# A host-transposed copy of x for the first stage of a spectral block: normalisation applied behind the row products

## The chip, the cores and the metric

The kernel runs on one core of a Trainium2 chip. The metric is the device time of one execution in microseconds (us), taken as the median of several runs. Five engines work from their own instruction queues: TensorE (PE in the profile; PEld are its weight loads), VectorE (DVE), ScalarE (ACT), GpSimd (POOL), and SyncE (SP), which here only issues DMAs. DMAs bring data from the chip's main memory into the on-chip buffer SBUF; matrix products land in PSUM, 8 banks of 128 x 512 fp32 numbers.

## The reference

A transformer-like block on `x` of 2048 rows of 512, all fp32. `mod` gives six vectors of 512 (shift, scale and gate of each half).

```
mod = (silu(c) @ w_mod).reshape(1, 6, 1, 512)
sa, ca, ga, sb, cb, gb = (mod[:, i] for i in range(6))
h = layernorm(x) * (1 + ca) + sa
x = x + ga * irfft2(rfft2(h) * (w_r + 1j * w_i))      # 2-D FFT over 2048 x 512
h = layernorm(x) * (1 + cb) + sb
x = x + gb * (mish(h @ w1 + b1) @ w2)                 # 512 -> 1376 -> 512
```

`layernorm` has no weights of its own: it subtracts the mean of a row and divides by the square root of its variance plus 1e-5.

## The kernel before

The Fourier transforms are products with constant matrices. Row `16 p + n` of `x` sits on partition `p` in tile `n`, so there are 16 tiles of 128 x 512. Three stages follow one another, with the dense half behind the third.

*First stage* (lines 242 to 347). Per tile: statistics on DVE (`norm_sums`, `bn_stats` and `bn_aggr`, L105 and L106); `norm_guess` adds epsilon on DVE (L111) and takes the root as Exp(-0.5 Ln) on ACT (L112, L113); `norm_refine` improves it by four small operations and forms minus mean times deviation (L118 to L126). `p1_apply` writes the normalised tile (ACT for the first three tiles, L160, else POOL, L162). `p1_turn` transposes it by four TensorE operations into a bank (L170), which ACT copies out as `ht` (L172). `p1_row` multiplies the four transposed blocks with the row matrix `krs` (L187; fp32, each counted as two instructions). ACT rounds the result to a high part `gh` (L190), DVE takes the rest `gl` (L191). `p1_split` does the same to the tile's column matrix: high part on ACT (L177), low part and negatives on POOL (L178, L179). `p1_col` is nine products of the split parts into one bank (L199 to L201), copied to `a_sb` by ACT (L202).

`krs` is the constant `kr` times one plus the scale `ca`: `scale_sums` (L207) sums `silu(c) @ w_mod` on TensorE from `wmc`, `scale_rows` (L212) multiplies on DVE. The shift `sa` goes the other way: `mod_step` (L90, L92) accumulates it on DVE from `wms`, `shift_columns` and `shift_rows` (L97, L222, L228, L230) turn it into `saz`, a correction of one column per group in the second stage. The gate `ga` is accumulated from `wmg` and multiplied into the inverse matrix `kiv` by `mod_gate` (L234, L235), the last work of the stage. `warm` (L240) runs products whose results nobody reads.

*Second stage* (lines 349 to 548). Seventeen groups of up to four frequencies: `p2_in` transposes `a_sb` (L431, copied by ACT, L434, corrected by `saz` on POOL, L436), `p2_mul` multiplies (L447), `p2_prod` multiplies by the filter `wq` on DVE (L463) and combines on POOL (L468, L469), `p2_back` transposes (L480, L483), `p2_out` multiplies (L493, L356, L357). One modulation step of the dense half (`mod_late`, twelve in all) runs on DVE in each of the rounds 1 to 12, on weights that `mod_fetch` brings two rounds ahead.

The order on each engine is the order in which the functions are called: the schedule is written by hand (`manual_schedule`). An engine works strictly in that order and waits on semaphores; SP issues its DMAs strictly in order too. Buffers come from rings: `bank` has two banks to each of four tags, `buf` two buffers to each tag; a writer waits until the last reader of the buffer it takes is done.

Of the kernel before, what the change touches and what calls it, by code (L numbers as in the profile page):

```python
# [12 lines left out]
P = 128  # L13
# [13 lines left out]
def tile_spectral_block(ctx: ExitStack, tc: tile.TileContext, x_d, w1_d, b1_d, w2_d,  # L27
                        c_d, wm_d, wq_d, wz_d, kr_d, km_d, kc_d, ki_d, kf_d, kv_d, kw_d, kp_d, out_d):
# [49 lines left out]
    wq = pw.tile([P, N2, 2, 64, 4], F32, name="wq")  # L78
# [5 lines left out]
    kw = pw.tile([32, 384], F32, name="kw")  # L84
    hring = first.enter_context(tc.tile_pool(name="hring", bufs=1))
# [30 lines left out]
    def norm_refine(lo, hi, ve, eng=nc.vector):  # L116
        r = rstd[:, lo:hi]
        eng.tensor_tensor(ve, ve, r, op=ALU.mult)  # L118
        eng.tensor_tensor(ve, ve, r, op=ALU.mult)
        eng.tensor_scalar(ve, ve, -0.5, 1.5, op0=ALU.mult, op1=ALU.add)  # L120
        eng.tensor_tensor(r, r, ve, op=ALU.mult)
        if eng is nc.vector:
            eng.scalar_tensor_tensor(nmr[:, lo:hi], mv[:, lo:hi, 0], -1.0, r, op0=ALU.mult, op1=ALU.mult)
        else:
            eng.tensor_tensor(nmr[:, lo:hi], mv[:, lo:hi, 0], r, op=ALU.mult)
            eng.tensor_scalar(nmr[:, lo:hi], nmr[:, lo:hi], -1.0, 0.0, op0=ALU.mult, op1=ALU.add)  # L126
# [30 lines left out]
    def p1_apply(n):  # L157
        h = buf(("h", "y", "t")[n % 3])
        if n < 3:
            nc.scalar.activation(h, x[:, n, :], AF.Identity, scale=rstd[:, n:n + 1], bias=nmr[:, n:n + 1])  # L160
        else:
            nc.gpsimd.tensor_scalar(h, x[:, n, :], rstd[:, n:n + 1], nmr[:, n:n + 1],  # L162
                                    op0=ALU.mult, op1=ALU.add)
        st["h", n] = h

    def p1_turn(n):
        hv = st.pop(("h", n)).rearrange("p (a b) -> p b a", b=4)
        pt = bank("A")
        for j in range(4):
            nc.tensor.transpose(pt[:, j * P:(j + 1) * P], hv[:, j, :], ident)  # L170
        ht = hring.tile([P, 4, P], F32, name="ht", tag="ht", bufs=4)
        nc.scalar.copy(ht.rearrange("p j s -> p (j s)"), pt)  # L172
        st["ht", n] = ht
# [8 lines left out]
    def p1_row(n):  # L182
        ht = st.pop(("ht", n))
        pg = bank("B")
        pgv = pg.rearrange("p (c d q) -> p d c q", c=2, d=4)
        for j in range(4):
            nc.tensor.matmul(pgv[:, j], ht[:, j, :], krs[:, j, :].rearrange("p (c q) -> p c q", c=2),  # L187
                             start=True, stop=True)
        gh, gl = buf("g1", F32R), buf("g2", F32R)
        nc.scalar.copy(gh, pg)  # L190
        nc.vector.tensor_tensor(gl, pg, plain(gh), op=ALU.subtract)  # L191
        st["g", n] = gh, gl

    def p1_col(n):
# [7 lines left out]
        nc.scalar.copy(a_sb[:, :, n, :], pa.rearrange("p (e q) -> p q e", e=8))  # L202
# [7 lines left out]
    def scale_rows(ps):  # L210
        for j in range(4):
            nc.vector.scalar_tensor_tensor(krs[:, j, :], kr[:, j, :], ps[j][:, 0:1], kr[:, j, :],  # L212
                                           op0=ALU.mult, op1=ALU.add)

# [17 lines left out]
    def mod_gate():  # L232
        ga = bank("B")
        nc.tensor.matmul(ga, ones, kr.rearrange("p j e -> p (j e)"), start=True, stop=True)  # L234
        nc.vector.tensor_tensor(kiv, kiv, ga.rearrange("p (b a) -> p b a", b=4), op=ALU.mult)  # L235

# [5 lines left out]
    with tc.manual_schedule():  # L242
        nc.scalar.dma_start(sc, c_d.rearrange("b (p k) -> p (b k)", k=4))
        for k in range(4):
            nc.scalar.dma_start(wmc[:, k, :], wm_d[:, 1, k, :])
        nc.scalar.preload_act_table_set("natural_log_exp_and_others")
        load_x(0)
        nc.sync.dma_start(ident, kp_d)
        load_x(1)
        nc.sync.dma_start(kr, kr_d)  # L250
        load_m(0)
        for n in range(2, N2):
            load_x(n)
            load_m(n - 1)
        load_m(N2 - 1)
        wmg = big.tile([P, 4, 512], F32, name="wmg", tag="cr")
        for w, i in ((wms, 0), (wmg, 2)):
            for k in range(4):
                nc.sync.dma_start(w[:, k, :], wm_d[:, i, k, :])
        nc.sync.dma_start(kf, kf_d)  # L260
        nc.sync.dma_start(wz, wz_d)
        for i in range(N2):
            nc.sync.dma_start(wq[:, i], wq_d[i])
            if i == 3:
                nc.sync.dma_start(kv, kv_d)
                nc.sync.dma_start(kw, kw_d)
# [7 lines left out]
        warm(12)  # L274
        norm_sums(0)
        norm_scale(0, 1)
        p1_apply(0)
        cps = [bank(t) for t in "DDCC"]
        for k in range(3):
            scale_sums((k,), cps)  # L280
            warm(1)
        p1_turn(0)
        scale_sums((3,), cps)
        norm_sums(1)
        ve = norm_guess(1, 2)
        norm_refine(1, 2, ve, nc.gpsimd)
        p1_split(0)
        p1_apply(1)
        scale_rows(cps)
        norm_sums(2)  # L290
        nc.sync.dma_start(kiv, ki_d)
        nc.sync.dma_start(b1n[:, 0:NF - 1], b1_d[0:(NF - 1) * P].rearrange("(f p) -> p f", p=P))
        nc.sync.dma_start(b1n[0:F - (NF - 1) * P, NF - 1:NF], b1_d[(NF - 1) * P:F].unsqueeze(1))
        p1_row(0)
        p1_turn(1)
        warm(3, "D")
        ve = norm_guess(2, 3)
        norm_refine(2, 3, ve, nc.gpsimd)
        norm_sums(3)
        p1_split(1)  # L300
        p1_row(1)
        p1_col(0)
        p1_apply(2)
        ve = norm_guess(3, 4)
        norm_refine(3, 4, ve, nc.gpsimd)
        p1_apply(3)
        norm_sums(4)
        p1_turn(2)
        p1_col(1)
        p1_split(2)  # L310
        norm_sums(5)
        norm_scale(4, 6)
        p1_turn(3)
        p1_apply(4)
        p1_apply(5)
        p1_row(2)
        p1_turn(4)
        p1_split(3)
        norm_sums(6)
        norm_sums(7)  # L320
        norm_scale(6, 8)
        p1_apply(6)
        for n in range(3, N2 + 1):
            if n < N2:
                p1_row(n)
            if n + 1 < N2:
                p1_split(n + 1)
            if n + 5 < N2:
                norm_sums(n + 5)
            if n % 2 == 0 and n + 5 < N2:  # L330
                norm_scale(n + 4, n + 6)
            if n >= 1:
                p1_col(n - 1)
            if n + 2 < N2:
                p1_turn(n + 2)
            if n + 4 < N2:
                p1_apply(n + 4)
            if 8 <= n < 12:
                mod_step(macc, wms[:, n - 8, :], n - 8, nc.vector)
            if n == 12:  # L340
                shift_columns()
            if n == 13:
                shift_rows()
            if 14 <= n < 16:
                for k in (2 * n - 28, 2 * n - 27):
                    mod_step(kr.rearrange("p j e -> p (j e)"), wmg[:, k, :], k, nc.vector)
        mod_gate()
# [532 lines left out]
```

## Time and profile before

| what | us |
|---|---|
| median of 3 runs (419.08 to 420.97) | 419.62 |
| profiled execution | 419.22 |
| its span, first to last instruction | 417.4 |
| first transposes of the second stage start at | 66.38 |
| first products of the third stage start at, about | 118.5 |

The profile is one execution. A line of a timeline reads: start, length, engine, source line, operation, output <- inputs, shape, how many were merged, and in brackets the idle time before it with what ended it. A group's line gives the count, the total busy time, the mean of one in ns, and the idle time before. Matrix products overlap in the pipeline, so their starts tell the pace better than their lengths.

### The profile page before, as it was taken

What the parts mean: (1) busy time and instruction counts of PE and PEld (TensorE: products, weight loads), DVE (VectorE), ACT (ScalarE), POOL (GpSimd) and SP (SyncE); (2) the same over time, 40 slices, a digit from 0 to 9 for tenths busy, and PEclk for the clock granted to TensorE, in tenths of its full rate; (3) what the DMA queues carried; (4) which work ended last, traced back from release to release, by engine and by line L of the source; (5) the groups of instructions that cost most, each with busy time, mean ns of one, the idle gap of its engine ahead of it and who ended that gap; (6) DMA issues with size and microseconds to landing.
All of it is one profiled execution on the core that took longest, in us unless ns stands there. A gap on an engine that the chain in (4) does not pass through costs nothing.

```text
span 417.4 us, 6112 instructions
## 1 busy us (share of the span) xinstructions
PE 404.8 (97%) x2343; PEld 350.6 (84%) x2343; DVE 185.9 (45%) x390; ACT 151.9 (36%) x338; POOL 90.1 (22%) x142
## 2 busy tenths in 40 slices
PE   8789999999999999999999999999999999999996
PEld 8679997899989999688878888878888878888874
DVE  3567855777417698635422423322423322422212
ACT  2566665467755653534311222211222211111110
POOL 0467661766503455222100000000000000000000
PEclk9999999999999999999999999999999999999999
DMA  8999520343032222111000200000200000200002
GB/s 271 332 320 344 170 77 25 103 146 160 0 94 69 70 68 80 48 53 50 19 2 0 101 2 0 2 0 0 102 0 0 2 0 2 101 0 2 0 0 101
DMA packets 18732, 30.39 MB, mean 73 GB/s; under 512 B 3472, under 2 KB 6320, under 8 KB 18448
## 3 DMA queue, kind: packets, MB, share of 16 engines
q1 hardware_dynamic: 17984, 28.96, 21.2%
q10 hardware_dynamic: 720, 1.05, 0.7%
q8 instruction: 18, 0.29, 0.3%
q14 instruction: 10, 0.08, 0.1%
HBM read 25.81 MB, written 4.19 MB: 72 GB/s over the span
## 4 chain that ended last, share of the span: by engine, by line
PE 85%; DMA 7%; DVE 3%; ACT 3%; issue 1%; POOL 1%; SPq 0%; DVEq 0%; POOLq 0%
PE bank L662 29%; PE bank L683 28%; PE bank L625 4%; PE bank L615 3%; PE bank L616 3%; PE bank L493 3%; DMA x<-in_A_x_dram 3%; PE bank L447 3%; PE bank L480 2%; PE bank L591 2%; DMA wmc<-in_w_mod_dram 1%; PE bank L431 1%; DMA wmg<-in_w_mod_dram 1%; PE bank L187 1%; PE bank L199 1%
## 5 line engine op out<-in xcount | busy, mean ns | idle before, releaser
L683 PE MATMUL bank<-w,ah 128*128 128x512 f32 (+1 forms) x352 | 108.8, 390 | 0.9 <-PE bank L662 0.9
L662 PE MATMUL bank<-h,w1h 128*128 128x512 f32 (+1 forms) x352 | 96.8, 398 | 0.0
L670 ACT ACTIVATE mw<-bank,b1n 128x512 f32<-128x512 f32 (+1 forms) x44 | 30.2, 688 | 181.2 <-PE bank L662 129.1
L671 DVE CAST ah<-mw 128x512 fp32r<-128x512 f32 (+1 forms) x44 | 20.1, 457 | 156.9 <-ACT mw L670 156.9
L683 PEld LDWEIGHTS bank<-w,ah 128*128 128x128 f32 (+1 forms) x352 | 66.1, 188 | 15.6 <-PE bank L662 1.3
L662 PEld LDWEIGHTS bank<-h,w1h 128*128 128x128 f32 (+1 forms) x352 | 65.0, 187 | 15.1
L683 PE MATMUL bank<-w,al 128*128 128x512 f32 (+1 forms) x176 | 68.6, 390 | 0.0
L662 PE MATMUL bank<-h,w1l 128*128 128x512 f32 (+1 forms) x176 | 48.2, 396 | 0.0
L662 PEld LDWEIGHTS bank<-h,w1l 128*128 128x128 f32 (+1 forms) x176 | 32.9, 187 | 8.1
L683 PEld LDWEIGHTS bank<-w,al 128*128 128x128 f32 (+1 forms) x176 | 33.0, 188 | 7.4 <-DVE al L672 0.4
L672 DVE TENSOR_TENSOR al<-mw,ah 128x512 fp32r<-128x512 f32 (+1 forms) x44 | 30.5, 692 | 4.5 <-PE bank L683 0.5
L615 PE MATMUL bank<-kc,d 128*128 128x128 f32 x128 | 24.9, 276 | 0.5 <-ACT d L356 0.5
L616 PE MATMUL bank<-kc,d 128*128 128x128 f32 x128 | 24.7, 275 | 0.0
L463 DVE TENSOR_TENSOR buf<-bank,wq 128x512 f32<-128x512 f32 (+1 forms) x32 | 20.2, 674 | 8.8 <-POOL buf L469 4.1
L105 DVE BATCH_NORM_STATS2 st<-x 128x6 f32<-128x512 f32 x32 | 22.0, 687 | 0.4
L638 POOL TENSOR_TENSOR buf<-buf,modr 128x512 f32<-128x512 f32 (+1 forms) x11 | 14.2, 1289 | 33.0 <-DMA buf<-in_B_w_dram 28.8
L571 POOL TENSOR_TENSOR w1l<-buf,w1h 128x512 fp32r<-128x512 f32 (+1 forms) x12 | 14.4, 1201 | 29.1 <-ACT w1h L570 29.0
L199 PE MATMUL bank<-buf,mring 128*128 128x512 f32 x48 | 20.3, 422 | 0.0
L615 PEld LDWEIGHTS bank<-kc,d 128*128 128x128 f32 x128 | 19.4, 192 | 0.7 <-ACT d L356 0.7
L616 PEld LDWEIGHTS bank<-kc,d 128*128 128x128 f32 x128 | 19.4, 192 | 0.0
L187 PE MATMUL bank<-modr,ht 128*128 128x128 f32 x128 | 17.4, 279 | 0.2 <-ACT ht L172 0.2
L625 PE MATMUL bank<-kiv,buf 128*128 128x128 f32 x128 | 17.2, 277 | 0.0
(141 smaller groups left out, 567.3 us busy)
## 6 DMA issues: line engine op xcount, KB each, us to landing
buf<-in_B_w_dram SPq DMA_DIRECT2D x18, 256.0 KB, 2.6
x<-in_A_x_dram SPq DMA_DIRECT2D x16, 256.0 KB, 4.4
wq<-in_w_q_dram SPq DMA_DIRECT2D x16, 256.0 KB, 4.9
out_dram<-x SPq DMA_DIRECT2D x16, 256.0 KB, 2.1
wm<-in_w_mod_dram SPq DMA_DIRECT2D x12, 256.0 KB, 2.8
mraw<-in_km_dram SPq DMA_DIRECT2D x16, 128.0 KB, 4.4
kc<-in_kc_dram SPq DMA_DIRECT2D x2, 1024.0 KB, 6.7
wmc<-in_w_mod_dram ACTq DMA_DIRECT2D x4, 256.0 KB, 6.0
```

Of the source, the lines that this page charges most:

```text
L105: nc.vector.bn_stats(t, x[:, n, :])
L187: nc.tensor.matmul(pgv[:, j], ht[:, j, :], krs[:, j, :].rearrange("p (c q) -> p c q", c=2), start=True, stop=True)
L199: nc.tensor.matmul(pa, m[:, a, 0:128], g, start=(i == 0), stop=False)
L463: nc.vector.tensor_tensor(tv, pbv, wt.unsqueeze(1).to_broadcast([P, 2, 64, nq]), op=ALU.mult)
L615: nc.tensor.matmul(o, dj[:, 0:128], kc[0][:, n, :], start=True, stop=False)
L616: nc.tensor.matmul(o, dj[:, 64:192], kc[1][:, n, :], start=False, stop=True)
L625: nc.tensor.matmul(px[:, j * P:(j + 1) * P], e[:, j * P:(j + 1) * P], kiv[:, j, :], start=True, stop=True)
L662: nc.tensor.matmul(ps, w[:, k, fs], h[:, k, :], start=(i == 0), stop=(i == 11))
L670: nc.scalar.activation(w, ps, AF.Mish, bias=b1n[:rows, g % NF:g % NF + 1])
L671: nc.vector.tensor_copy(ah, w)
L672: nc.vector.tensor_tensor(al, w, plain(ah), op=ALU.subtract)
L683: nc.tensor.matmul(out_ps[b][j], a[:, j * P:(j + 1) * P], w2[f // 6][:rows, f % 6, w, :], start=(f == 0 and i == 0), stop=(f == NF - 1 and ...
```

## The change

The host hands over a second copy of `x`, `x_t`, in which each tile is already transposed (16 tiles of 128 x 4 x 128). Row products run on that raw copy. Mean and deviation, which belong to a row of `x` and so to a partition of the result, are applied behind the product: `row_sums` forms once the row products of ones, `kb`; per tile DVE computes `c = kb * mean - product` (`p1_mean`), ACT `gh = c * r` rounded, and DVE `gl = c * r - gh` (`p1_low`), with `r` the deviation taken with a minus sign (`p1_scale`). The statistics still read the untransposed tile. Transposes, their copies and the applies are gone. Row products run two tiles ahead of column products, and the copy to `a_sb` (`p1_save`) is called one tile later.

Around it: the transposed tiles stand in a ring of eight (`xring`), and loads of tile `n + 10` are called behind the row products of tile `n + 2`; the second half of the filter (`wqb`) takes the ring's memory and is loaded at the start of the second stage; constants of the second stage are loaded after tile 15 (`load_rest`); `wmc` comes in two DMAs instead of four, `wms` in one instead of four. The shift is accumulated by ACT and POOL (`shift_sum`) instead of DVE; `shift_rows` stands behind the last tile. The gate `ga` and `mod_gate` move into the second stage, whose modulation steps are now sixteen, some rounds with two; its first two `p2_mul` are called later (behind six and seven `p2_in` instead of three and four), and DVE does the subtraction of `p2_prod` for the first three and the last two groups, POOL every addition.

```
-    wq = pw.tile([P, N2, 2, 64, 4], F32, name="wq")
+    wqa = pw.tile([P, 8, 2, 64, 4], F32, name="wqa")
+    xring = pw.tile([P, 8, 4, P], F32, name="xring", tag="half")
+    kb = modr[:, 2]
...
+    def p1_scale(lo, hi, eng):
+        ve = norm_guess(lo, hi)
         r = rstd[:, lo:hi]
         eng.tensor_tensor(ve, ve, r, op=ALU.mult)
         eng.tensor_tensor(ve, ve, r, op=ALU.mult)
+        eng.tensor_scalar(ve, ve, 0.5, -1.5, op0=ALU.mult, op1=ALU.add)
         eng.tensor_tensor(r, r, ve, op=ALU.mult)
...
-    def p1_apply(n):
-    def p1_turn(n):
...
+    def load_xt(n):
+        t = xring[:, n % 8]
+        nc.sync.dma_start(t, xt_d[n])
+        st["xt", n] = t
+    def load_all(n):
+        load_xt(n)
+        load_x(n)
+        load_m(n)
+    def load_rest():
+        nc.sync.dma_start(ident, kp_d)
+        nc.sync.dma_start(kf, kf_d)
+        nc.sync.dma_start(wz, wz_d)
+        for i in range(8):
+            nc.sync.dma_start(wqa[:, i], wq_d[i])
+            if i == 2:
...
+    def row_products(pg, data):
         pgv = pg.rearrange("p (c d q) -> p d c q", c=2, d=4)
         for j in range(4):
+            nc.tensor.matmul(pgv[:, j], data(j), krs[:, j, :].rearrange("p (c q) -> p c q", c=2),
                              start=True, stop=True)
+    def p1_row(n):
+        xt = st.pop(("xt", n))
+        st["pg", n] = pg = bank("AB"[n % 2])
+        row_products(pg, lambda j: xt[:, j, :])
+    def row_sums():
+        ps = bank("D")
+        row_products(ps, lambda j: ones)
+        nc.scalar.copy(kb, ps)
+    def p1_mean(n):
+        c = buf("hy"[n % 2])
+        nc.vector.scalar_tensor_tensor(c, kb, mv[:, n, 0:1], st.pop(("pg", n)), op0=ALU.mult, op1=ALU.subtract)
+        gh = buf("g1", F32R)
+        nc.scalar.activation(gh, c, AF.Copy, scale=rstd[:, n:n + 1])
+        st["g", n] = c, gh
+    def p1_low(n):
+        c, gh = st.pop(("g", n))
+        gl = buf("g2", F32R)
+        nc.vector.scalar_tensor_tensor(gl, c, rstd[:, n:n + 1], plain(gh), op0=ALU.mult, op1=ALU.subtract)
         st["g", n] = gh, gl
...
+    def shift_sum(k):
+        t = macc if k == 0 else buf("t")
+        nc.scalar.activation(t, wms[:, k, :], AF.Copy, scale=sc[:, k:k + 1])
+        if k:
+            nc.gpsimd.tensor_tensor(macc, macc, t, op=ALU.add)
...
+        load_xt(0)
+        nc.sync.dma_start(kr, kr_d)
         load_x(0)
         load_m(0)
+        for n in range(1, 8):
+            load_all(n)
...
+        warm(14)
         norm_sums(0)
+        p1_scale(0, 1, nc.vector)
         cps = [bank(t) for t in "DDCC"]
+        for k in range(4):
             scale_sums((k,), cps)
+            if k == 1:
+                warm(4)
+        scale_rows(cps)
+        p1_split(0)
+        p1_row(0)
+        load_all(8)
+        row_sums()
+        p1_row(1)
+        load_all(9)
         norm_sums(1)
+        p1_scale(1, 2, nc.gpsimd)
+        p1_mean(0)
         p1_split(1)
         p1_split(2)
+        for n in range(N2):
+            if n >= 1:
+                p1_save(n - 1)
+            if n + 2 < N2:
+                p1_row(n + 2)
+                if n + 10 < N2:
+                    load_all(n + 10)
+                if n == 4:
+                    nc.sync.dma_start(wms, wm_d[:, 0, :, :])
+                if n == 6:
+                    load_rest()
             if n + 1 < N2:
+                p1_mean(n + 1)
+            p1_low(n)
+            if n == N2 - 1:
                 shift_columns()
+            p1_col(n)
+            if n + 3 < N2:
+                p1_split(n + 3)
+            if n == 0:
+                norm_sums(2)
+            if n + 3 < N2:
+                norm_sums(n + 3)
+                if n % 2 == 0:
+                    p1_scale(n + 2, n + 4, nc.gpsimd if n else nc.vector)
+            if 10 <= n < 14:
+                shift_sum(n - 10)
+        p1_save(N2 - 1)
+        shift_rows()
...
-        eng = nc.vector if g == seq[-1] else nc.gpsimd
+        eng = nc.vector if g in (*seq[:3], *seq[-2:]) else nc.gpsimd
         eng.tensor_tensor(y[:, 0:u], pr[0][:, 0:u], pr[1][:, u:w], op=ALU.subtract)
-        eng.tensor_tensor(y[:, u:w], pr[0][:, u:w], pr[1][:, 0:u], op=ALU.add)
+        nc.gpsimd.tensor_tensor(y[:, u:w], pr[0][:, u:w], pr[1][:, 0:u], op=ALU.add)
...
+    when = (3, 4, 5, 6, 6, 7, 8, 9, 9, 10, 11, 12, 12, 13, 14, 15)
+    for i, s in enumerate(when):
+        work_mod[s].append((i // 4, (0, 1, 0, 2)[i // 4], nc.vector, i % 4))
...
+        for i in range(8):
+            nc.sync.dma_start(wqb[:, i], wq_d[8 + i])
         for i in range(LEAD):
             p2_in(seq[i])
-            if i in (2, 3):
-                p2_mul(seq[i - 2])
+            if i in (5, 6):
+                p2_mul(seq[i - 5])
...
+            if s == 7:
+                mod_gate()
```

More of the change, by code (lines that the diff above doesn't have):

```diff
@@ L155, in load_x @@
         nc.sync.dma_start(x[:, n:n + 1, :], xv[:, n:n + 1, :])
-    def p1_apply(n):
[L158 to L164, printed above, removed]
-    def p1_turn(n):
[L167 to L173, printed above, removed]
+    def load_xt(n):
[13 more added lines that the diff above has]
+            if i == 2:
+                nc.sync.dma_start(kv, kv_d)
+                nc.sync.dma_start(kw, kw_d)
+                nc.sync.dma_start(kiv, ki_d)
+                nc.sync.dma_start(b1n[:, 0:NF - 1], b1_d[0:(NF - 1) * P].rearrange("(f p) -> p f", p=P))
+                nc.sync.dma_start(b1n[0:F - (NF - 1) * P, NF - 1:NF], b1_d[(NF - 1) * P:F].unsqueeze(1))
     def p1_split(n):
@@ L519, in mod_shift, with mod_gate @@
             nc.scalar.copy(cols[:, 1, i, :], ps[:, 0:4])
+    def mod_gate():
+        ga = bank("A")
+        nc.tensor.matmul(ga, ones, modr[:, 0], start=True, stop=True)
+        nc.vector.tensor_tensor(kiv, kiv, ga.rearrange("p (b a) -> p b a", b=4), op=ALU.mult)
     kc = []
+    wqb = pw.tile([P, 8, 2, 64, 4], F32, name="wqb", tag="half")
     with tc.manual_schedule():
[L523 removed]
+        for i in range(8):
+            nc.sync.dma_start(wqb[:, i], wq_d[8 + i])
         for i in range(LEAD):
             p2_in(seq[i])
[L526 to L527 removed]
+            if i in (5, 6):
+                p2_mul(seq[i - 5])
         for s in range(len(seq) + 3):
```

140 lines of the change are left out of this document (22 added, 118 removed).

## The prediction

> **What bounds the kernel now.** I read the page first, then the stretches of the first 32 us, then TensorE's timeline through the first stage. From the page:
>
> ```profile
> span 417.4 us, 6112 instructions
> PE 404.8 (97%) x2343; PEld 350.6 (84%) x2343; DVE 185.9 (45%) x390; ACT 151.9 (36%) x338; POOL 90.1 (22%) x142
> x<-in_A_x_dram SPq DMA_DIRECT2D x16, 256.0 KB, 4.4
> mraw<-in_km_dram SPq DMA_DIRECT2D x16, 128.0 KB, 4.4
> ```
>
> TensorE is busy 97% of the span, so time is won only where its work shrinks or where it stands idle. The busy time of each engine in stretches of 4 us (first column: the stretch, its length; last two: DMA share, GB/s):
>
> ```profile
> 12.00:16.00 4.00, 2.45 (x19) 2.07 (x18) 2.25 (x6) 2.22 (x7) 2.08 (x8) 1.00 0.93 320
> 16.00:20.00 4.00, 2.61 (x19) 2.27 (x19) 2.64 (x9) 2.48 (x7) 2.25 (x8) 1.00 1.02 354
> 20.00:24.00 4.00, 3.32 (x25) 2.96 (x24) 0.89 (x4) 2.37 (x6) 2.97 (x9) 1.00 0.97 328
> 24.00:28.00 4.00, 2.75 (x21) 2.49 (x20) 3.36 (x9) 1.50 (x4) 2.35 (x4) 1.00 0.93 296
> 28.00:32.00 4.00, 4.00 (x33) 3.82 (x32) 3.37 (x10) 2.93 (x8) 2.76 (x5) 1.00 1.01 366
> ```
>
> From 12 to 28 us TensorE is idle 4.87 us of 16; from 28 on it is full. Its timeline, with one tile of the full part and the end of the stage:
>
> ```profile
> 21.58 0.28 PE L201 MATMUL bank<-buf,mring 128*128 128x256 f32 x1
> ...
> 28.32 0.65 PE L170 MATMUL bank<-ident,buf 128*128 128x128 f32 x4
> 28.82 1.06 PE L187 MATMUL bank<-modr,ht 128*128 128x128 f32 x8
> 29.63 0.48 PE L199 MATMUL bank<-buf,mring 128*128 128x512 f32 x1
> ...
> 31.12 0.65 PE L170 MATMUL bank<-ident,buf 128*128 128x128 f32 x4
> ...
> 54.62 0.95 PE L97 MATMUL bank<-ones,modr 128*128 128x1 f32 x8
> 55.44 1.14 PE L187 MATMUL bank<-modr,ht 128*128 128x128 f32 x8
> ...
> 58.32 1.06 PE L222 MATMUL bank<-kr,cols 128*128 128x128 f32 x8
> 59.21 1.06 PE L187 MATMUL bank<-modr,ht 128*128 128x128 f32 x8
> ...
> 65.42 1.12 PE L234 MATMUL bank<-kr,ones 128*128 128x512 f32 x2
> 66.38 1.72 PE L431 MATMUL bank<-ident,a_sb 128*128 128x128 f32 x11
> ```
>
> Tile 1's column products end at about 21.8, tile 2's only at 28.3; then a tile takes 2.80 us (28.32 to 31.12): transposes 0.50, row products 0.81, column products 1.49. The second stage starts at 66.38. Reading starts, not busy times, matters: the ends overlap.
>
> **Start.** The shift is worked from these rows:
>
> ```profile
> 6.35 1.52 PE L207 MATMUL bank<-sc,wmc 128*128 128x128 f32 x8
> ...
> 10.63 1.06 PE L207 MATMUL bank<-sc,wmc 128*128 128x128 f32 x8
> 11.06 1.16 DVE L212 SCALAR_TENSOR_TENSOR modr<-kr,bank 128x128 f32<-128x128 f32 x4 [1.39 <-PE bank L207]
> 11.84 0.19 POOL L118 TENSOR_TENSOR ve<-ve,rstd 128x1 f32<-128x1 f32 x1 [11.38 <-ACT rstd L113]
> 12.11 0.19 POOL L119 TENSOR_TENSOR ve<-ve,rstd 128x1 f32<-128x1 f32 x1
> ```
>
> The modulation sums still start near 6.35. Transposes no longer stand among them, but four warm products do; the 1 MB of `wmc` and the 0.78 MB ahead of `mraw` on SP come at 0.33 MB/us, hence by 8 to 9.5. I take 10.6 for the first `scale_rows` (0.5 earlier; bounds 10.2 to 11.3). Row products of tile 0 end at 12.1, `row_sums` (new, another 0.9) at 13.0, its ACT copy to `kb` at 13.8. Then `c(0)` on DVE to 14.5, `gh(0)` on ACT to 15.4, `gl(0)` to 16.15; statistics of tiles 2 and 3 to 17.75, `ve`, Ln and Exp (0.2 each, L113 below, and two hand-overs) to 18.55, four refining operations on DVE at 0.2 (POOL's start 0.27 apart) to 19.4 and `c(2)`, `gl(1)` to 20.8. Column products of tile 1 end 0.6 later, 21.4: no better than now. But rows and means run ahead, so the hole of tile 2 (21.8 to 28.3) is not repeated.
>
> **The steady tile.** TensorE keeps 0.81 + 1.49 = 2.30 us. DVE gets two products a tile for one; POOL loses the apply, ACT the copy of the transposes. From DVE's timeline, the answer on line 111 (shortest, median, longest ns) and the groups of the stage (busy, then mean ns of one):
>
> ```profile
> 29.92 0.68 DVE L105 BATCH_NORM_STATS2 st<-x 128x6 f32<-128x512 f32 x1
> 30.63 0.18 DVE L106 BATCH_NORM_AGGREGATE mv<-st 128x2 f32<-128x6 f32 x1
> 30.73 0.66 DVE L191 TENSOR_TENSOR buf<-bank,buf 128x512 fp32r<-128x512 f32 x1
> 31.30 0.68 DVE L105 BATCH_NORM_STATS2 st<-x 128x6 f32<-128x512 f32 x1
> ...
> 51.61 0.74 DVE L92 SCALAR_TENSOR_TENSOR modr<-wms,sc,modr 128x512 f32<-128x512 f32 x1
> 52.28 0.68 DVE L191 TENSOR_TENSOR buf<-bank,buf 128x512 fp32r<-128x512 f32 x1
> ```
> ```profile
> L111 DVE TENSOR_SCALAR ve<-mv x15: 142/170/700, 7.1 to 169.5; 128x2 f32<-128x2 f32 x8, 128x1 f32<-128x1 f32 x4, 128x4 f32<-128x4 f32 x3
> ```
> ```profile
> L178 POOL TENSOR_TENSOR mring<-mraw,mring 128x256 fp32r<-128x256 f32 x16 | 12.3, 766 | 4.8 <-ACT mring L177 4.8
> L202 ACT COPY a_sb<-bank 128x512 f32<-128x512 f32 x16 | 9.4, 588 | 4.5 <-PE bank L201 4.4
> L177 ACT CAST mring<-mraw 128x256 fp32r<-128x256 f32 x16 | 6.8, 424 | 0.0
> L179 POOL TENSOR_SCALAR mring<-mring 128x256 fp32r<-128x256 f32 x16 | 6.6, 411 | 1.5
> L113 ACT ACTIVATE rstd<-rstd 128x2 f32<-128x2 f32 x6 | 1.2, 204 | 0.2
> L160 ACT ACTIVATE buf<-x,nmr,rstd 128x512 f32<-128x512 f32 x3 | 2.4, 815 | 2.4 <-POOL nmr L126 1.4 <-DVE nmr L123 1.0
> ```
>
> By starts: statistics 0.81 (29.92 to 30.73). `c`, a scalar-tensor-tensor with one PSUM input, between 0.57 (L191) and 0.67 (L92): 0.62. `gl`, two SBUF inputs, 0.67 undisturbed, up to the 0.85 of the mean in the second stage (row below): 0.70. `ve` once a pair, 0.14 to 0.70: 0.2 a tile. Sum 2.33, bounds 2.1 to 2.7. ACT: 0.59 + 0.82 (L160 bounds `gh` above, L202 below) + 0.42 + 0.2 = 2.0, with `shift_sum` on tiles 10 to 13 up to 2.9, absorbed because `gh` is a tile ahead of `gl`. POOL: 0.77 + 0.41 + 0.55 = 1.7. DVE and TensorE are level, so they will miss each other at times: I take 2.45 a tile (2.30 to 2.8). The pair's loop of the deviation, statistics to `ve` to ACT (0.5) to four POOL operations at 0.27 (11.84 to 12.11) to `gh` to `gl`, sums to 0.81 + 0.4 + 0.6 + 1.1 + 0.9 + 0.7 = 4.5 against 4.9 for two tiles: it just fits.
>
> **End of the stage.** `gl(12)` ends at 20.8 + 11 x 2.45 = 47.75, its columns 0.6 later; tile 13 takes 2.30, tile 14 (no row left) 1.49, `shift_columns` 0.82 (54.62 to 55.44) and tile 15 1.49: 54.45. `shift_rows` is moved behind it, 0.89 (58.32 to 59.21), and covers the last save. Second stage at 55.4, so 66.38 - 55.4 = **11.0 us won**. With 2.30 and 2.8 a tile: 12.6 and 7.1.
>
> **Second stage.** `mod_gate` is moved, not removed: 0.96 (65.42 to 66.38) comes back between full products. Four more modulation steps go to DVE:
>
> ```profile
> 80.00:84.00 4.00, 4.00 (x38) 4.00 (x37) 2.51 (x5) 2.53 (x8) 1.15 (x4) 1.00 0.28 78
> L92 DVE SCALAR_TENSOR_TENSOR modr<-wm,sc,modr 128x512 f32<-128x512 f32 x9 | 7.6, 849 | 0.0
> ```
>
> TensorE is full there and DVE has 1.5 us free in 4, so the 4 x 0.85 and the differences moved from POOL are mostly hidden; groups with two steps are not quite, and I charge 0.5 (0 to 2). The fill starts with six groups of transposes before its first product, paced by the ACT copies, and its waits for `saz` (reductions now just ahead) are covered by them; the subtraction on DVE takes POOL's turn out. I take these as even (-1 to +1).
>
> **Queues.** SP now carries per tile 0.64 MB (two rows of 256 KB, one of 128), 1.95 us at 0.33 MB/us: below 2.45, and eight tiles are issued before the ring makes SP wait for a row product. Tile 3 lands near 14, needed at 17. `wms` (1 MB) and the 2.8 MB behind it follow tile 15's load at about 30 and land by 42. The eight `wqb` loads wait for the last row product (near 49), 2 MB, by 58; behind them on SP stand only fetches needed after 62, and `wqb` itself is read after 75. All this is off the path; a delay of one tile at the start would cost 2.
>
> The sum: -11.0 + 0.96 + 0.5 = **-9.5**. The profiled execution took 419.22, 1.8 outside its span; that is 0.4 under the median, 419.62, from which I subtract: **410.1**.
>
> **A rule against it.** L111 takes 0.14 at its shortest and 0.70 at its longest: something holds DVE up. The Trainium skill, "SBUF — State Buffer", section "Who interferes with whom", says that a VectorE operation with two SBUF inputs and a GpSimd operation that reads SBUF exclude each other for a whole instruction; until now the low part had one input in PSUM, now both are in SBUF. By L92, which has such inputs and takes 0.74 in the first stage and 0.85 on average in the second, the trace shows little of it; its price is the first rival's.
>
> **Rivals.** (1) *DVE and POOL block each other.* `gl` waits each time for the POOL operation in progress: half of 0.77, or all of it. A tile becomes 2.8 to 3.1, times 12 tiles: +4 to +8, **414 to 418**. For: L111's 0.70. Against: L92's means. (2) *Slower: the deviation loop becomes the period.* If `ve` is held 0.7, POOL's four operations queue behind a split (1.18) and `gh` behind a save and a cast (1.0), the loop is 4.5 + 0.3 + 1.2 + 1.0 = 7.0 a pair: 3.5 a tile, 12 x 1.05 = +12.6, **422.7**. It decides from 6.6 a pair on. Against: those operations are issued in an order in which the split goes first. (3) *TensorE alone bounds*, 2.30 a tile and an even fill: **408**. (4) *It does not do what it says*: the second stage is not ready earlier, because `saz`, `ident` or the late loads hold it; then the 11 us turn into a wait at its door and the time stays within 2 us, **419**. Against: the loads end by 42 at the rate shown.
>
> **Chances.** Forecast (408.5 to 413) 0.57; rival 1 0.20; rival 3 0.09; rival 4 0.05; rival 2 0.09. A measurement here tells 0.5% (2.1 us) from no change. Faster takes the forecast, rival 3 and most of rival 1: 0.84; same 0.07; slower 0.09. The range, 407.3 to 416.0, takes in rival 3 and three quarters of rival 1 and leaves out the rest of it and rivals 2 and 4: 0.19. The forecast's own is 408.5 to 413.
>
> **What would show it.** Right: no transposes before the second stage, whose first one starts at 55 to 56; TensorE's column products of tile 2 end before 25; a tile of 2.3 to 2.5 with DVE about 95% busy; `gl` near 0.72. Wrong: `gl` or L178's successor over 0.9 (rival 1); ACT waiting on POOL for `gh` in every pair (rival 2); TensorE idle 2 us or more between the last column product and the first transposes (rival 4); the start of the first row product after 12.

## The result and the profile after

The changed kernel takes **417.73 us** in the median of twenty executions (414.65 to 419.40); the kernel before took 419.16 on the same chips. The ratio, which goes by averages and not by the two medians, is 0.9951, with an interval of 0.9936 to 0.9967: a gain clear of the noise but small, 1.4 us by the medians, where 9.5 were forecast.

The execution that was profiled is the fastest of the twenty, 414.65 us. So there are two questions: why this one won 4.6 us and not 9.5, and why most executions are 3 us longer than it. First the page of the changed kernel, and its engines in stretches of 4 us (columns as before, the granted clock third from the end):

```profile
span 412.7 us, 5968 instructions
PE 397.7 (96%) x2287; PEld 343.1 (83%) x2287; DVE 192.1 (47%) x377; ACT 146.3 (35%) x322; POOL 87.6 (21%) x139
```
```profile
20.00:24.00 4.00, 2.94 (x21) 2.77 (x22) 3.93 (x8) 2.62 (x5) 1.55 (x3) 1.00 0.99 347
24.00:28.00 4.00, 4.00 (x31) 3.77 (x31) 3.93 (x9) 2.57 (x7) 2.45 (x7) 1.00 1.01 364
...
52.00:56.00 4.00, 1.90 (x12) 1.53 (x10) 1.25 (x2) 2.27 (x4) 3.37 (x8) 1.00 0.94 284
```

TensorE lost 7.1 us of work (404.8 to 397.7), and looks full from 24 us on instead of 28. But a new gap stands at the end of the stage, in 52 to 56, and POOL is the busiest engine there. TensorE's timeline names the places:

```profile
10.90 1.26 PE L196 MATMUL bank<-modr,xring 128*128 128x128 f32 x8
...
21.06 0.50 PE L227 MATMUL bank<-buf,mring 128*128 128x512 f32 x1 [2.28 <-DVE buf L219]
...
21.63 1.05 PE L196 MATMUL bank<-modr,xring 128*128 128x128 f32 x8
...
23.93 1.05 PE L196 MATMUL bank<-modr,xring 128*128 128x128 f32 x8
...
33.83 1.05 PE L196 MATMUL bank<-modr,xring 128*128 128x128 f32 x8
...
39.05 1.05 PE L196 MATMUL bank<-modr,xring 128*128 128x128 f32 x8
...
54.50 0.50 PE L227 MATMUL bank<-buf,mring 128*128 128x512 f32 x1 [2.10 <-ACT buf L213]
...
56.65 1.05 PE L99 MATMUL bank<-ones,modr 128*128 128x1 f32 x8 [0.39 <-POOL modr L250]
...
59.06 1.05 PE L259 MATMUL bank<-kr,cols 128*128 128x128 f32 x8
59.95 2.27 PE L424 MATMUL bank<-ident,a_sb 128*128 128x128 f32 x15
```

The start is as forecast: row products from 10.90, a hole of 2.28 at tile 1, none at tile 2. The first tiles then take 2.30 to 2.37 each (21.63 to 23.93 is one). From the column products of tile 6 on, a pair of tiles takes 5.22 us (33.83 to 39.05 is one), not 4.6 or 4.9; the busy time hides this, since the ends overlap the waits, and the starts tell it. Tile 14 waits 2.10 us. The second stage starts at 59.95: 6.4 us won in place of 11.0.

**The loop that sets 5.22.** All engines through one pair, from a `gh` that waits for POOL to the next such `gh`, and on to the next `ve`:

```profile
31.53 0.72 ACT L213 ACTIVATE buf<-buf,rstd 128x512 fp32r<-128x512 f32 x1 [1.65 <-POOL rstd L132]
...
32.16 0.39 ACT L188 CAST mring<-mraw 128x256 fp32r<-128x256 f32 x1
...
32.62 1.01 POOL L189 TENSOR_TENSOR mring<-mraw,mring 128x256 fp32r<-128x256 f32 x1 [1.13 <-ACT mring L188]
...
33.73 0.41 POOL L190 TENSOR_SCALAR mring<-mring 128x256 fp32r<-128x256 f32 x1
...
33.89 0.26 DVE L113 TENSOR_SCALAR ve<-mv 128x2 f32<-128x2 f32 x1
...
34.10 0.73 POOL L189 TENSOR_TENSOR mring<-mraw,mring 128x256 fp32r<-128x256 f32 x1
...
34.43 0.20 ACT L115 ACTIVATE rstd<-rstd 128x2 f32<-128x2 f32 x1
...
34.72 0.74 DVE L219 SCALAR_TENSOR_TENSOR buf<-buf,rstd 128x512 fp32r<-128x512 f32 x1
...
34.92 0.81 POOL L190 TENSOR_SCALAR mring<-mring 128x256 fp32r<-128x256 f32 x1
...
35.69 0.19 POOL L129 TENSOR_TENSOR ve<-ve,rstd 128x2 f32<-128x2 f32 x1
...
36.53 0.20 POOL L132 TENSOR_TENSOR rstd<-rstd,ve 128x2 f32<-128x2 f32 x1
...
36.76 0.72 ACT L213 ACTIVATE buf<-buf,rstd 128x512 fp32r<-128x512 f32 x1 [1.65 <-POOL rstd L132]
...
37.51 0.75 DVE L219 SCALAR_TENSOR_TENSOR buf<-buf,rstd 128x512 fp32r<-128x512 f32 x1 [0.60 <-ACT buf L213]
...
38.18 0.69 DVE L107 BATCH_NORM_STATS2 st<-x 128x6 f32<-128x512 f32 x1
...
39.12 0.26 DVE L113 TENSOR_SCALAR ve<-mv 128x2 f32<-128x2 f32 x1
```

Read first the ring that the deviation goes round: `ve` 33.89, root on ACT done at 34.63, four operations on POOL from 35.69 to 36.73, `gh` at 36.76, `gl` at 37.51, statistics at 38.18, the next `ve` at 39.12. That is 5.23 us, and 1.06 of it is the stretch from 34.63 to 35.69, in which POOL still works on the split (L189, L190) that stands ahead of the four operations in its queue. A ring with a wait in it does not set the pace. The one without runs through POOL: `gh` at 31.53, the cast behind it on ACT at 32.16, the first split of the pair on POOL at 32.62 (it had waited for that cast), the second at 34.10, the four operations from 35.69, and the next `gh` at 36.76, 5.23 later. Two queues close it: the cast stands behind `gh` on ACT, and the four operations stand behind both splits on POOL.

Two of its operations are stretched while a `gl` runs on DVE (at 34.72, and by the timeline at 32.29): L189 takes 1.01 against 0.73 at 34.10, L190 takes 0.81 against 0.41 at 33.73. Without these 0.68 us the ring would be 4.55 by these rows, an estimate, just under the 4.59 of two tiles on TensorE. So the order of the queues and the stretching set the 5.23 together.

**The end.** POOL and ACT ahead of `gh(14)`:

```profile
49.77 1.29 POOL L250 TENSOR_TENSOR modr<-modr,buf 128x512 f32<-128x512 f32 x1
51.01 1.20 POOL L189 TENSOR_TENSOR mring<-mraw,mring 128x256 fp32r<-128x256 f32 x1
52.30 0.41 POOL L190 TENSOR_SCALAR mring<-mring 128x256 fp32r<-128x256 f32 x1
52.66 0.20 POOL L129 TENSOR_TENSOR ve<-ve,rstd 128x2 f32<-128x2 f32 x1
```

The deviation of tile 14 is ready on ACT at 50.56 (L115 there, by the timeline); POOL reaches it at 52.66, behind an addition of `shift_sum` (L250, 1.29) and a split lengthened to 1.20. By the timeline 6.53 us pass from `gh(12)` (47.20) to `gh(14)` (53.73), 1.30 more than the ring's 5.23: one addition. The rest of the hole is the ring's own, since TensorE has no row products left to do between these tiles and arrives earlier.

### The profile page after: what moved, and what is told of

Its sections match the earlier page's. It is cut to its first block, busy times and chain, and to the rows that moved or that the text cites. A ratio compares the mean times of both kernels' runs of the same rounds, so it can differ in the third digit from the quotient of the medians.

```text
span 412.7 us, 5968 instructions
## 1 busy us (share of the span) xinstructions
PE 397.7 (96%) x2287; PEld 343.1 (83%) x2287; DVE 192.1 (47%) x377; ACT 146.3 (35%) x322; POOL 87.6 (21%) x139
## 4 chain that ended last, share of the span: by engine, by line
PE 87%; DVE 4%; POOL 3%; issue 2%; ACT 1%; DMA 1%; POOLq 0%
PE bank L664 30%; PE bank L685 29%; PE bank L627 4%; PE bank L617 4%; PE bank L618 3%; PE bank L440 3%; PE bank L486 3%; PE bank L593 2%; PE bank L473 2%; PE bank L272 2%; PE bank L424 1%; PE bank L196 1%; POOL mring L189 1%; DVE buf L456 1%; POOL mring L190 1%
## 5 line engine op out<-in xcount | busy, mean ns | idle before, releaser
L227 PE MATMUL bank<-buf,mring 128*128 128x512 f32 x48 | 20.8, 433 | 6.4 <-ACT buf L213 3.9
L189 POOL TENSOR_TENSOR mring<-mraw,mring 128x256 fp32r<-128x256 f32 x16 | 13.9, 867 | 18.0 <-ACT mring L188 18.0
L196 PE MATMUL bank<-modr,xring 128*128 128x128 f32 x128 | 16.9, 276 | 0.0
```

Source lines behind the costliest of these rows:

```text
L189: nc.gpsimd.tensor_tensor(m[:, 1, 0:256], mraw[:, n, :], plain(m[:, 0, 0:256]), op=ALU.subtract)
L196: nc.tensor.matmul(pgv[:, j], data(j), krs[:, j, :].rearrange("p (c q) -> p c q", c=2), start=True, stop=True)
L227: nc.tensor.matmul(pa, m[:, a, 0:128], g, start=(i == 0), stop=False)
```

## The experiments

All kernels but the unaltered one are edits of the changed kernel; each was compared with the kernel before on its chip. Ratios are to that kernel.

**Unaltered, twice.** Edit: none.

> The changed kernel once more, unaltered. Its profiled execution (414.65) is the fastest of twenty whose median is 417.73; that of before lies at its own median. Theory D (data arrive late in typical executions): a typical execution shows the same pace of tiles from 30 us on, but a longer wait for x tiles or their transposed copies ahead of it, or a second stage that waits for wqb or wm. Theory J (the loop itself jitters): the same arrivals, but pairs of tiles longer than 5.2 us or a longer stall ahead of tile 14's column products (2.1 in the profile shown). Expected 417 to 418 by both; the profile tells which.

> The changed kernel unaltered, beside the next three on one chip. Theory C (holes lower the clock): median 416 to 418, mean clock mostly 0.984 to 0.996, times rising as the clock falls. Rival H (chips differ, filling does nothing): the same times as the kernels with filled holes on this chip, within 0.6 us.

The first gave 415.96 us (414.67 to 420.36, ten executions), ratio 0.9932 (0.9900 to 0.9963); the second, on another chip, 417.56 (415.37 to 417.81, seven), ratio 0.9953 (0.9935 to 0.9970). Both have pairs of 5.22 us, so theory J falls. Of theory D the first one's profile (415.69) shows a start that waits for data, with row products 0.6 us later (11.50); the typical execution of the second has not even that (10.53). What goes with the time from one execution to the next is the mean granted clock of TensorE: in the first, 414.7 at 0.999 to 1.000, 415.7 to 416.0 at 0.995, 416.9 to 417.9 at 0.986 to 0.988, 420.4 at 0.984. The twenty of the result line up in the same way: 414.65 at 0.999, a cluster of 417.3 to 417.9 mostly at 0.985 to 0.986. The kernel before has no such cluster; the means of its executions stand at 0.994 to 1.000. The stretches of the second, whose profile is a typical execution (417.56):

```profile
20.00:24.00 4.00, 3.28 (x16) 3.05 (x17) 3.90 (x10) 2.62 (x5) 1.87 (x3) 0.72 1.05 371
24.00:28.00 4.00, 4.00 (x28) 3.77 (x27) 3.86 (x8) 2.35 (x6) 2.46 (x6) 0.86 1.04 338
...
56.00:60.00 4.00, 4.00 (x16) 3.60 (x16) 1.35 (x2) 1.25 (x3) 0.94 (x1) 0.50 0.96 347
60.00:64.00 4.00, 3.87 (x22) 3.44 (x21) 0.85 (x2) 1.14 (x3) 0.00 (x0) 0.66 0.40 153
```

Right behind each of the two holes (2.28 us to 20.72 and 2.11 us to 54.83 in this timeline) the clock falls, to half at the lowest, and TensorE passes 16 products in 56 to 60, where the next kernel below passes 26 at full clock. Its second stage starts at 62.92, which is 52.39 us behind its first row products, against 49.05 in the fastest execution (59.95 and 10.90). A theory that holes cost only their own length has no place for this.

**The holes filled with unread products.** Both holes:

```
             for i, (a, g) in enumerate(...)       # inside p1_col
+                if n == 1 and i == 2:
+                    warm(9, "D")
...
+            if n == 14:
+                warm(9, "D")
             p1_col(n)
```

> The changed kernel with nine products nobody reads in each of its two holes of over 2 us (ahead of the last third of tile 1's column products and ahead of tile 14's). Theory C (the holes lower the granted clock in part of the executions, which costs the 3 us between the fastest execution, 414.65, and the median, 417.73): the mean granted clock is 0.997 or more in every execution, all of them end at 414.3 to 415.5, the fastest is not faster. Rival D (arrival of data, clock only an accompaniment): the clock rises but the times stay spread, median above 416.5.

> Both holes filled, as before on another chip. Theory C: median 414.2 to 415.2, clock 0.997 or more in nearly all executions, 1.5 to 3 us below the unaltered kernel on the same chip. Rival H: within 0.6 us of it.

414.48 us (414.21 to 414.68), ratio 0.9892 (0.9877 to 0.9907), and beside the unaltered kernel on the same chip 414.72 (414.18 to 414.97), ratio 0.9893 (0.9880 to 0.9906): 2.8 us below that one's 417.56, with intervals that do not touch. Its stretches:

```profile
20.00:24.00 4.00, 3.72 (x30) 3.40 (x29) 3.93 (x9) 2.43 (x5) 1.28 (x3) 1.00 0.96 318
...
56.00:60.00 4.00, 3.58 (x26) 3.17 (x25) 1.44 (x3) 1.65 (x5) 1.31 (x1) 1.00 0.87 300
```

The clock was 0.998 to 1.000 in all eight executions of the two runs, though the second stage started no earlier than in the profiled execution of the result: 49.06 us behind the first row products, against 49.05. So work that nobody reads buys 2.8 us: the clock is the cause of the distance between the fastest and the usual execution.

**One hole alone**, by two sizes of filler: the first hole by nine products (or five and four in two banks), the late one likewise.

> Products nobody reads only in the late hole (ahead of tile 14), the hole of tile 1 as it is. By theory C each hole costs where it meets the clock's decision. If the late hole is the dear one, since the end of the stage and the second stage's start follow it: clock 0.995 or more in nearly all executions, median 414.5 to 415.2. If the hole of tile 1 is the dear one: clock 0.985 to 0.996 as before, median above 416.

> Only the hole of tile 1 filled. Theory C with the late hole as the dear one: clock 0.985 to 0.996, median within 0.7 us of the unaltered kernel. With the early hole as the dear one: median 1 us or more below it.

> Only the hole ahead of tile 14 filled (the kernel whose median was 418.15 on another chip). With the late hole as the dear one: 1 us or more below the unaltered kernel here, so that the 418.15 was the chip's; else within 0.7 us of it or above.

> Only the hole of tile 1 filled, but by two takings of a bank (five and four products), so that the rotation of the two D banks behind it is that of the unaltered kernel and of the one with both holes filled. If the rotation made the wait at the head of the dense half (2.8 to 3.1 us with one taking, 0.9 to 1.4 with none or two), it is back under 1.5. Then the cost of the late hole alone shows: median 415.5 to 417, clock 0.992 to 0.996 in those executions that lose. If not, the wait stays near 3 and the median above 417.5.

> Only the hole ahead of tile 14 filled, again by two takings. Same test of the rotation: wait at the dense half under 1.5. Then the cost of the early hole alone: median 415 to 416, clock about 0.996 in those executions that lose (3 to 4 us at a lower clock around 20 to 28 us).

The late one: 418.15 (ratio 0.9967, 0.9954 to 0.9981), again 417.50 (0.9959, 0.9946 to 0.9973), with five and four 418.29 (0.9959, 0.9940 to 0.9979). The first: 418.53 (0.9988, 0.9963 to 1.0014), with five and four 418.65 (0.9968, 0.9940 to 0.9996). None gained on the unaltered kernel (417.56 on the chip of the runs with 417.50 and 418.53). The profiles show why they can't be read as prices of one hole: all five have a new wait of 2.8 to 3.2 us at the head of the dense half (near 168 us), with a drop of the clock behind it, where the result's profile waits 1.4 and the kernel with both filled 0.9 and 1.1. With the first hole filled:

```profile
PE bank L687 <- issue: 2.8, 1, 2.8
```
```profile
168.00:172.00 4.00, 1.17 (x4) 0.63 (x3) 2.54 (x8) 2.82 (x5) 1.27 (x1) 0.86 0.14 54
```

The runs with five and four products tried the idea that an odd number of banks taken shifts the later rotation; the wait stayed, so that idea falls. The timelines show what is late there: the fourth of POOL's products with the gate of the dense half (L642 in this kernel) comes after a wait of 2.2 to 2.7 us in all five, and of 1.1 to 1.6 in the unaltered kernels and those with both holes filled. Behind it stand a cast on ACT, a split and the next statistics on DVE, and then on ACT the root and a table load of 1.28, ahead of the activation that TensorE waits for. Why that product is late is open.

The price of each hole by itself these kernels don't give, but for one execution a timeline does. In the typical one (417.56), counted from the first row products and set against the fastest, 1.6 us are lost right behind the first hole, of which 0.7 are left at the column products of tile 10, since tiles that wait for POOL take in the rest. Another 2.65 are lost from there to the second stage, behind the late hole.

**The shift back on DVE.**

```
-                shift_sum(n - 10)
+                mod_step(macc, wms[:, n - 10, :], n - 10, nc.vector)
```

> The shift is accumulated on DVE again (four steps at the same places), POOL's three additions and ACT's four scalings go. Theory Q (POOL's queue): the additions of 1.3 us delay the last splits and deviations, so the 2.1 us stall before tile 14 and most of the wait before shift_columns go, and the second stage starts 2.5 to 3.5 us earlier: ratio to before lower by 0.006 to 0.008 than the unaltered kernel's. Theory P (port exclusion alone): DVE's own steps have two SBUF inputs as well, so about as much is lost to them: within 0.002 of the unaltered kernel.

414.63 us (414.30 to 416.07), ratio 0.9893 (0.9856 to 0.9929). Pairs stay at 5.22. Its first row product came 0.8 late in the profiled execution (11.69), its second stage at 59.85: 0.9 earlier against that start, well under the 2.5 to 3.5 of theory Q. The interval overlaps that of the unaltered kernel on the same chip (0.9900 to 0.9963), so the gain over it is not clear by the times. The hole at tile 14 falls from 2.10 to 0.74, but DVE, with another modulation step in each of four tiles, now holds up two more (0.67 and 0.63). The addition moves from one full engine to another.

**The split behind the deviation.**

```
             p1_col(n)
             if n + 3 < N2:
-                p1_split(n + 3)
...
                     p1_scale(n + 2, n + 4, nc.gpsimd if n else nc.vector)
+                p1_split(n + 3)
```

> p1_split(n+3) is called behind p1_scale, so POOL does the deviation ahead of the split of that round. Theory Q: two tiles fall from 5.22 us to DVE's own 4.6 to 4.8, five pairs, 2 to 3 us earlier second stage. Theory P: gl and the splits still exclude each other, two tiles stay above 5.0, gain under 0.7 us.

415.67 us (413.98 to 417.12), ratio 0.9909 (0.9876 to 0.9942), which again overlaps the unaltered kernel's; the pace of the tiles tells more. Its timeline of TensorE and the groups of its first 60 us, which are set against those of the next experiment:

```profile
36.61 1.05 PE L196 MATMUL bank<-modr,xring 128*128 128x128 f32 x8
...
38.91 1.05 PE L196 MATMUL bank<-modr,xring 128*128 128x128 f32 x8
...
55.02 1.48 PE L99 MATMUL bank<-ones,modr 128*128 128x1 f32 x8 [2.08 <-POOL modr L250]
```
```profile
L189 POOL TENSOR_TENSOR mring<-mraw,mring 128x256 fp32r<-128x256 f32 x16 | 14.3, 894 | 11.1 <-ACT mring L188 11.1
...
L219 DVE SCALAR_TENSOR_TENSOR buf<-buf,rstd 128x512 fp32r<-128x512 f32 x16 | 13.5, 846 | 1.9 <-ACT buf L213 1.0 <-PE bank L229 0.8
```

With four small operations no longer behind a split, tiles take 2.30 to the end of the loop, although the stretched operations stay long: without this order there is no pair of 5.22. (That it takes the stretching as well shows in the next experiment.) The end of the stage does not profit: the additions pile up on POOL instead, `shift_columns` waits 2.08 for them, and behind that wait the clock of this execution is 0.50 (56 to 60). Its second stage starts at 60.77, with a lower clock behind the first hole too (0.67 in 20 to 24); the execution to hold it against is the typical one of the unaltered kernel, with 62.92.

**`c` in PSUM.**

```
-        c = buf("hy"[n % 2])
+        c = bank("D")
```

> c is written to PSUM (the two banks of tag D, idle in the loop) instead of SBUF, so gl has one SBUF input. Theory P: gl falls from a mean of 0.81 to 0.70, POOL's low product from 0.87 to 0.75 and its negation from 0.51 to 0.41, two tiles from 5.2 to 4.7 us; the second stage starts 1.5 to 3 us earlier. Theory Q: the durations may fall, but the order on POOL stays, two tiles stay within 0.3 us of 5.2, and the stall at tile 14 stays above 1.5.

411.52 us (411.03 to 413.99), ratio 0.9824 (0.9781 to 0.9867), clear of the unaltered kernel's on the same chip (415.96 us there). `gl` now has one input in SBUF and one in PSUM. The groups of the first 60 us, of the result and of this kernel:

```profile
L189 POOL TENSOR_TENSOR mring<-mraw,mring 128x256 fp32r<-128x256 f32 x16 | 13.9, 867 | 18.0 <-ACT mring L188 18.0
L219 DVE SCALAR_TENSOR_TENSOR buf<-buf,rstd 128x512 fp32r<-128x512 f32 x16 | 13.0, 811 | 5.5 <-ACT buf L213 5.3
...
L190 POOL TENSOR_SCALAR mring<-mring 128x256 fp32r<-128x256 f32 x16 | 8.1, 507 | 1.4
...
L113 DVE TENSOR_SCALAR ve<-mv 128x2 f32<-128x2 f32 (+1 forms) x9 | 2.1, 228 | 0.3
```
```profile
L219 DVE SCALAR_TENSOR_TENSOR buf<-bank,rstd,buf 128x512 fp32r<-128x512 f32 x16 | 11.9, 743 | 1.8 <-ACT buf L213 1.7
L189 POOL TENSOR_TENSOR mring<-mraw,mring 128x256 fp32r<-128x256 f32 x16 | 11.8, 735 | 18.1 <-ACT mring L188 17.6
...
L190 POOL TENSOR_SCALAR mring<-mring 128x256 fp32r<-128x256 f32 x16 | 6.5, 408 | 1.4
...
L113 DVE TENSOR_SCALAR ve<-mv 128x2 f32<-128x2 f32 (+1 forms) x9 | 4.1, 455 | 0.3
```

One edit of DVE's input takes 0.13 us off POOL's first split operation, 0.10 off the second and 0.07 off `gl`: the two engines had held each other up. `ve` now meets the split instead and doubles. The order of the queues is unaltered here, and still pairs take 4.81 (35.58 to 40.39 in its timeline), the holes at the end are 0.32, 0.83 and 0.36, and the second stage starts at 56.71.

**Both together, and the shift with them.** Shift on DVE and late split; then `c` in PSUM with these; then late split, `c` in PSUM and `shift_sum` on POOL two tiles earlier (`if 8 <= n < 12: shift_sum(n - 8)`):

> Both edits on the order of POOL together: the split behind the deviation, and the shift accumulated by DVE; c stays in SBUF. Theory Q (POOL's queue is the whole of the late second stage): pairs of tiles at 4.6 us, no stall over 1 us after tile 2, second stage at 56 to 57, median 411 to 413. Theory P (the exclusion by itself keeps it late): DVE, with two operations of two SBUF inputs a tile in the last tiles, falls behind, second stage after 58.5, median above 414.

> The same two edits and c in PSUM. If queue and exclusion are two parts of one loop, either remedy already brings the pair to 4.6 to 4.8 and the second adds at most 1 us: second stage at 55 to 56.5, median 410 to 411.5. If they are separate costs the gains add: median below 409.5.

> Split behind the deviation, c in PSUM, and the shift still summed by ACT and POOL but two tiles earlier (tiles 8 to 11). By the account of the last tiles (POOL's additions of 1.3 us delay the last deviations and shift_columns) no stall over 1 us is left behind tile 2 and TensorE bounds: pairs at 4.6, second stage at 55 to 56, median 409.5 to 411. If DVE is the bound instead, pairs stay at 4.8 and the second stage starts at 56 to 57.

411.67 us (ratio 0.9822, 0.9807 to 0.9837), 410.96 (0.9825, 0.9796 to 0.9855) and 410.57 (0.9800, 0.9785 to 0.9815), with second stages at 56.50, 56.13 and 56.41. Pairs are 4.59 in all three, which is two tiles of TensorE; in the last a hole of 1.37 stays at tile 14, where none over 1 us was expected. The remedies do not add: each takes a part out of one ring, and once the ring is shorter than 4.6 us the rest of its waits cost nothing.

**The shift earlier, alone.**

> The changed kernel with one edit: shift_sum on tiles 8 to 11 instead of 10 to 13. If POOL's additions delay the last deviations, the 2.1 us stall ahead of tile 14 and the wait ahead of shift_columns go, and the second stage starts 2 to 3 us after where c in PSUM and the late split have it: near 57.5 to 58.5, with pairs of tiles still at 5.2 or longer where the additions now fall. If the last tiles are held by something else, it stays at 59.5 to 60.

418.27 us (417.30 to 419.06), ratio 0.9970 (0.9957 to 0.9983): a miss. The stalls come earlier (1.21 us at tile 12, 2.11 at tile 14), the second stage at 63.98, with the clock at 0.64 and 0.50 in 56 to 64. In a ring that POOL's queue already sets, there is no tile in which the additions are free; in the kernel with the late split and `c` in PSUM the pairs stay at 4.59 with the additions on the same tiles.

**One more step on the best.** Late split, `c` in PSUM, earlier shift, and the statistics of tile 2 ahead of the first `c`:

```
+        norm_sums(2)
         p1_mean(0)
...
-            if n == 0:
-                norm_sums(2)
```

> The best kernel so far (c in PSUM, split behind the deviation, shift on tiles 8 to 11) with the statistics of tile 2 ahead of the first c, where DVE waits 1.1 us for kb. If that wait takes them in, the hole of tile 1 shrinks by 0.8 us and so does the time: median 409.6 to 410.0. If x tile 2 has not landed by 13 us, or the first c is pushed back, no gain: 410.4 to 410.8.

**410.30 us** (409.94 to 411.72), ratio 0.9794 (0.9774 to 0.9814): the lowest median of all, below both kernels, though not to be told from the 410.57 of the kernel that it edits (another chip, overlapping intervals). The hole of tile 1 is 1.95 us where that kernel has 2.43, 0.5 less and not 0.8. Its rows keep their pace nearly to the end of the stage:

```profile
23.74 1.05 PE L196 MATMUL bank<-modr,xring 128*128 128x128 f32 x8
...
42.09 1.05 PE L196 MATMUL bank<-modr,xring 128*128 128x128 f32 x8
...
50.79 0.50 PE L227 MATMUL bank<-buf,mring 128*128 128x512 f32 x1 [1.38 <-ACT buf L213]
...
55.50 2.27 PE L422 MATMUL bank<-ident,a_sb 128*128 128x128 f32 x15
```

Eight tiles from 23.74 to 42.09 are 2.29 each.

## Why the prediction was right and wrong

**Right: the direction, the start, what is full.** First `scale_rows` at 10.44 by the timeline (10.6 said), row products of tile 0 done at 12.00 (12.1), `gl(1)` at 20.26 to 20.9 (20.8), no second hole, tiles of 2.30 where nothing else holds, `gh` and `gl` near their prices. `mod_gate` took 0.96 by starts, as said. The second stage lasted 53.4 us (59.95 to 113.35) for 52.1 before, 1.3 more for the 1.46 charged.

**Wrong: "it just fits".** The step that failed is the deviation loop of a pair, summed to 4.5 us against 4.9. Its terms were not short: without the wait for POOL the ring is 5.23 - 1.06 = 4.17. What was left out is that its four operations stand behind both splits of the pair in POOL's queue, and the first split behind `gh` and a cast in ACT's; that ring, with two operations stretched by `gl`, is 5.23. The second rival described nearly this, and its sign, ACT waiting on POOL for `gh` in every pair, is in the rows (1.65). But it priced the loop at 7.0 and got 0.09, on the argument that the split is issued first; being first is what makes it the obstacle. The ring lasted 0.6 us over TensorE's 4.6 a pair, and only from tile 6 on. By `gl(12)`, which ended at 48.7 and not 47.75, it had cost 0.9 us.

**Wrong: `shift_sum` "absorbed".** Only ACT's part was charged. POOL's three additions of 1.3 us fall on the engine that sets the ring, in the last three tiles. From `gl(12)` to the second stage 11.25 us passed, 7.65 in the sum. Of these 3.6 us more, about 2.0 are the additions, as read from the timeline: 1.30 between `gh(12)` and `gh(14)`, and by starts 0.66 ahead of `shift_columns`. About 1.6 are the ring again: tiles 13 and 14 were summed at TensorE's pace, but `gh(14)` comes a turn of the ring behind `gh(12)`. No run takes the additions away without putting work elsewhere, so this division is argued and not shown.

Together the second stage came 4.55 us late, which is the distance of the profiled execution (414.65) from 410.1; the terms behind it even out. With the split late, `c` in PSUM, the shift earlier and the start shortened, the second stage began at 55.50 (55.4 said), and the time was 410.30. That this meets the forecast is in part chance: its tiles take 2.29 and not 2.45, and a hole of 1.38 at the end takes much of that back.

**Rival 1, blocking, is real but was put in the wrong place.** It put all the cost on `gl`, 4 to 8 us. `gl` rose to 0.81, L178's successor L189 to 0.87, and the price came through POOL's queue. The edit that removes it won more than any other single one (4.4 us by the medians on one chip). That 417.73 lies in this rival's 414 to 418 is luck: 3.1 us of it are the clock. The Trainium skill, "SBUF — State Buffer", section "Who interferes with whom", states the rule that the prediction weighed; the groups above agree with it (L189 0.867 to 0.735 us, when DVE's second input moved to PSUM). L92's means were weak evidence against it: in the stretch of the second stage that the prediction shows, POOL had 1.15 us of 4 to do.

**Not thought of: the clock.** The sum knows a hole by its length and puts what follows it at nothing. Holes of 2.1 to 2.3 us also lowered the clock behind them in most executions, which is the step from 414.65 to 417.73, 3.1 us; filling both gave 2.8 us back on one chip. So the median lies 7.6 us over the 410.1: 4.55 from the ring and the additions, 3.1 from the clock. Rivals 3 and 4 fell: TensorE was not alone the bound, and the second stage started right behind the last work of the first (59.06 to 59.95).

## What to carry to other kernels

A chain that returns through several engines is priced with what stands ahead of it in each queue, not with its own operations; lay the queues of the engines side by side for one period and look for bulk work in front of small work that others wait for. An operation that is moved to an idle-looking engine is free only if that engine is not in such a ring in that stage. And where TensorE is nearly always full, a hole of 2 us can have a price beyond its length; look at the granted clock behind it before judging a median by a profile.

## What the hardware showed that was not expected

*The clock after short holes.* Holes of 2.28 and 2.11 us were followed by granted clocks of 0.72 and 0.50 in the next 4 us; the kernel before, whose longest hole in this stage is 1.5 us, kept means of 0.994 to 1.000 over whole executions, and the best version, with 1.95 and 1.38, kept 1.000 in four of five. Whether a given hole meets the drop varies: the profiled execution of the result had both holes and a clock of 1.00 behind them. The Trainium skill, "TensorE: Matmul & The Clock Gate", section "HAM oscillation — how this bites in real kernels", asks for no idle gaps above about 3.4 us; here shorter ones were enough, and the measurement decides. Half the clock as the lowest value agrees with that page.

*Blocking reaches small operations.* With `gl` out of the way, `ve`, 128 x 2 numbers and one input, went from 0.23 to 0.46 us on average, beside the same split on POOL: at 28.31 of that timeline it takes 0.53 and ends with the split (28.08, 0.73).
